# Second chunk of the second layer in seven products, two kinds of transform in attend's bank, folds dealt over more steps

## The chip, the cores and the metric

The kernel runs on one core of one Trainium2 chip. The metric is the device time of one execution in microseconds (us), the median of three runs; less is better. Times that belong to single instructions come from one further execution, which was recorded by the hardware profiler.

## The reference

Two blocks follow each other. The first is attention with a top-k mask over 8 batches, 8 heads, 576 tokens and 64 elements a head; the second mixes tokens and channels by a two-dimensional Fourier transform and then applies a two-layer perceptron. All values are fp32.

```python
scores = scale * np.matmul(q, k.transpose(0, 1, 3, 2))
kth = np.partition(scores, -32, axis=-1)[..., -32:-31]
scores = np.where(scores >= kth, scores, -1e9)
attn = softmax(scores)
x = (attn @ v) as (batch, token, 8 heads * 64)
mixed = np.real(np.fft.fft(np.fft.fft(x, axis=1), axis=2))
u = x + mixed
un = (u - mean(u)) / np.sqrt(var(u) + 1e-06)
out = u + np.maximum(un @ w_ch1, 0.0) @ w_ch2
```

Here w_ch1 is 512 x 2048 and w_ch2 is 2048 x 512.

## The kernel before, in words

**Steps.** The order of all engines' work is written out by a planner in the kernel and kept as written. The unit is a step, and each step i handles one attention tile (128 queries of one head, or the 64 last queries of two heads): there are 9 tiles for a pair of heads, 36 for a batch, 288 in all. A step issues, in this order on PE: scores of tile i+3 (L338, L353, L368), sometimes transposes of q or k (L282), sometimes the transposes of finished output to tokens (tpx, L512), the planned transforms ("pe1", "pe2", "pe"), the transposes of the probabilities of tile i-2 (tpP, L435 and L446), and at certain steps attend (o, L472). Between these pieces PE gets units of the perceptron from a queue, as many as level() and the planner's costs allow; a unit is at most eight or sixteen matmuls. ACT copies scores out of PSUM, makes half of the mask (relu, L405) and the exponential (L414), and copies the transposed probabilities (L438). DVE finds the 32 largest scores by four rounds of MAX8 (L389) and MATCH_REPLACE8 (L391). POOL makes the bounds nt of a tile (L398) and the other half of the mask (a subtraction, L408). In a step POOL's order is: the subtraction, the operations planned under "pool0" (folds), sums that wait in a list (some_sums), the bounds, further sums, and then what is planned under "pool" and "pool2". For pool0 the planner counts 1.5 us an operation; the sums before the bounds get what is left of 2.1 us, and those after it 1.3 us.

**Transforms.** When a batch's attention is complete, its x is folded (sums and differences of mirrored tokens and channels, fold_ops, on POOL for batches 1 to 6), transformed along the tokens (half_of_tokens: yp, L663, two halves g2 for each of two parities), copied to y by ACT (L694 and after), transformed along the channels (dft_channels: mp, L720 and L724, one for each of the five token tiles t), copied to us by ACT (L741), added to x by POOL (L747), measured by DVE (L752), scaled by 1/sqrt (rsqrt, DVE and POOL) and transposed for the perceptron (tpu, L789). The steps of these are set at the end of the kernel from T0, a few steps after the batch's last tile. The transforms of one batch so fall into the steps in which the perceptron of the batch before is finishing.

**Perceptron.** The tokens of a batch are two chunks: chunk 0 holds tiles 0, 1 and the tail tile 4, chunk 1 holds tiles 2 and 3. For each chunk hidden() makes relu(un @ w1) into a tile hT (L874, L878), 16 units. The second layer then has two forms. back() (L901) is the plain one: for a 128-token tile 16 matmuls of 512 columns, in 8 units. fast() is a Strassen-Winograd scheme for the two full tiles of a chunk: seven products p2, p1, p5, p4, p6, p3, p7, each 8 matmuls of 256 columns in two parts (product, L1071). An fp32 matmul of the program appears as two MATMUL instructions in the trace. The operands are mixtures of halves of hT ("21", "11", "12", "22", made by POOL in two halves each, L1016) and of w2, kept in DRAM and brought over by 512 KB transfers (bring, L817, on the queue of SP). The results alternate between the two halves of two PSUM banks named v and w. Of the results the first five are scaled by ACT into spare space (L1041) and added to x by POOL (L1043), the last two are added by DVE (L1029). POOL's mixes and adds stand in the list of sums; need() flushes them up to the one that a product requires. In the kernel before, chunk 0 of batches 1 to 6 and both chunks of batch 7 use fast(); everything else uses back().

**PSUM.** Of eight banks, scores have two (ps_s), transposes two (ps_t), attend and tpx share one (ps_o), and three (ps_m) are handed round by bank(): to hidden, back, the products, yp, mp and tpu. A product's bank is held until its last result is read. In batch 7 yp, mp and tpu use the banks of the attention.

Of the kernel before, what the change touches and what calls it, by code (L numbers as in the profile page):

```python
# [72 lines left out]
def kernel(  # L73
# [55 lines left out]
    def bank(shape, name, hold=False):  # L129
        n = banks_free.pop(0)  # L130
        t = ps_m.tile(shape, F32, name=name, tag=f"m{n}", bufs=1)
        if not hold:
            banks_free.append(n)
            return t
        return t, lambda: banks_free.append(n)

    ident = const.tile([P, P], F32, name="ident", tag="ident")
    fs = const.tile([P, 2, 2, 3, KQ], F32, name="fs", tag="fs")
# [468 lines left out]
    def fold_ops(b, par, eng, space="own"):  # L607

        x = x_of[b]

        if space == "hT":
            sp = batp.tile([P, NIT * CW[0]], F32, name=f"fsp_{b}", tag="hT")

        def buf(n, name, cols=DM):
            if space == "hT":
                return sp[:, 2 * DM * n:2 * DM * n + 2 * cols].rearrange("p (s c) -> p s c", s=2)
            pool, tag = (batp, ("fold_s", "fold_d")) if space == "own" else (attp, ("PT0", "PT1"))
            return pool.tile([P, 2, cols], F32, name=f"{name}_{b}_{par}", tag=tag[n % 2], bufs=1)  # L620

        got = folded[b, par] = []

        def first():
            got.append(buf(0, "sd"))
            op = ALU.add if par == 0 else ALU.subtract
            eng.tensor_tensor(out=got[0], in0=x[:, 0:2, :], in1=x[:, 2:4, :], op=op)

        def second():
            got.append(buf(1, "zw"))  # L630
            fold_halves(eng, got[0], got[1])

        def third(n):
            if n == 0:
                got.append(buf(2, "fg", DM + Q2))
            fold_channels(eng, got[1], got[2][:, :, 0:DM], got[2][:, :, DM:DM + Q2], n)

        def both():
            third(0)
            third(1)  # L640

        return [first, second, both, lambda: third(2)]

    def dft_tokens(b, par):
        for g2 in range(2):
# [3 lines left out]
    def half_of_tokens(b, par, g2):  # L649

        while any(u[2] == "hidden" for u in queue):
            one_unit()
        _, zw, fg = folded[b, par]
        if b not in y_of:
            y_of[b] = batp.tile([P, 4, S], F32, name=f"y_{b}", tag="y")
        y = y_of[b]
        shape, name = [P, 2, KQ], f"yp_{b}_{par}_{g2}"

        yp = ps_t.tile(shape, F32, name=name, tag="tp") if b == B - 1 else bank(shape, name)

        def mm(gg, st, lhsT, rows, table, start=False):

            nc.tensor.matmul(  # L663
                yp[rows, gg, :],
                lhsT=lhsT,
                rhs=fs[:, table, par, st, :],
                start=start,
                stop=st == 2,
                skip_group_check=True,
            )  # L670


        for gg in range(2):
            g = 2 * g2 + gg
            for st in range(3):
                f = fg[:, st] if st < 2 else ftail
                first = gg == 0 and st == 0
                if g2:
                    mm(gg, st, f[:, P * g:P * (g + 1)], slice(0, P), gg, first)
                    continue  # L680
                for h in range(2):
                    c0 = P * g + P // 2 * h
                    mm(gg, st, f[:, c0:c0 + P // 2], slice(P // 2 * h, P // 2 * (h + 1)), h, first)
        if g2 == 0:
            for st in range(3):
                f, c = (fg[:, st], DM + Q0) if st < 2 else (ftail, DM)
                mm(0, st, f[:, c:c + 1], slice(Q0, Q0 + 1), 0)

        mir, back = (
            (slice(HS + 2, S, 2), slice(KQ - 2, 0, -1)) if par == 0  # L690
            else (slice(HS + 1, S, 2), slice(KQ - 2, None, -1))
        )
        y2 = y[:, 2 * g2:2 * g2 + 2, :]
        nc.scalar.copy(out=y2[:, :, par:HS + 1:2], in_=yp[:, :, 0:KQ - par])  # L694
        if g2:
            nc.scalar.copy(out=y2[:, 0, mir], in_=yp[:, 0, back])
        else:
            nc.scalar.mul(out=y2[:, 0, mir], in_=yp[:, 0, back], mul=sg[:, 0:1])
        nc.scalar.mul(out=y2[:, 1, mir], in_=yp[:, 1, back], mul=sg[:, 1 + g2:2 + g2])
        if par == 1 and g2 == 1:  # L700
            tails_of_y(b)
# [6 lines left out]
    def dft_channels(b, t, quick=False):  # L708

        rows, y = ROWS[t], y_of[b]  # L710
        shape, name = [P, 2, DM // 2], f"mp_{b}_{t}"
        mp = ps_s.tile(shape, F32, name=name, tag="sp") if b == B - 1 else bank(shape, name)
        def of(g):
            if t == 4:
                return yt_of[b][:, g].rearrange("p h r -> p (h r)")
            k0 = HS * (t // 2) + P * (t % 2)
            return y[:, g, k0:k0 + P]

        for g in range(2):
            nc.tensor.matmul(  # L720
                mp[0:rows, 0, g:DM // 2:2], lhsT=of(g), rhs=fd[:, g], start=True, stop=True
            )
        for g in range(2, 4):
            nc.tensor.matmul(  # L724
                mp[0:rows, 1], lhsT=of(g), rhs=fd[:, 2 * g - 2:2 * g],
                start=(g == 2), stop=(g == 3),
            )
        if quick:
            xt = two(x_of[b][0:rows, t, :])
            at(now[0], "dve", lambda: nc.vector.tensor_tensor(  # L730
                out=xt, in0=mp[0:rows], in1=xt, op=ALU.add
            ))
            at(now[0], "dve", lambda: stats(b, t))
            return 1.75
        key = (b, t > 1 and t < 4)
        if key not in us_of:
            us_of[key] = batp.tile(
                [P, 2 if key[1] else 3, DM], F32, name=f"us_{b}_{t}", tag="fold_d" if key[1] else "fold_s"
            )
        us = us_of[key][0:rows, CHUNKS[int(key[1])].index(t), :]  # L740
        nc.scalar.copy(out=two(us), in_=mp[0:rows])  # L741
        return 1.75
# [117 lines left out]
    def mlp_units(b):  # L860
# [4 lines left out]
        def hidden(ch, it):  # L865
            w, unT = CW[ch], unT_of[b, ch]
            if ch not in hTs:
                hTs[ch] = batp.tile([P, NIT, CW[0]], F32, name=f"hT_{b}_{ch}", tag="hT")
                hT_of[ch] = hTs[ch].rearrange("p i c -> p (i c)")[:, 0:NIT * w].rearrange(
                    "p (i c) -> p i c", c=w  # L870
                )
            hp = bank([P, CW[0]], f"hp_{b}_{ch}_{it}")
            for dt in range(NDT):
                nc.tensor.matmul(  # L874
                    hp[:, 0:w], lhsT=w1[:, dt, P * it:P * (it + 1)], rhs=unT[:, dt, 0:w],
                    start=(dt == 0), stop=(dt == NDT - 1),
                )
            nc.scalar.activation(out=hT_of[ch][:, it, :], in_=hp[:, 0:w], func=AF.Relu)  # L878
# [10 lines left out]
        def ct_tile():  # L889
            if not cts:  # L890
                cts.append(batp.tile([P, 3, DM], F32, name=f"ct_{b}", tag="fold_s"))
            return cts[0]
# [83 lines left out]
        def fast(ch):  # L976
# [22 lines left out]
                }  # L999

            def room(n):
                return ct_tile().rearrange("p t c -> p (t c)")[:, DH * n:DH * (n + 1)]

            def later(key, us, fn, soon=False):
# [17 lines left out]
            def to_x(t, cols, src, n, then=lambda: None):  # L1022
# [4 lines left out]
                if n is None or last:  # L1027
# [9 lines left out]
                    else:  # L1037
                        late_next.append(add)
                    return
                r = room(n)  # L1040
                nc.scalar.mul(out=r, in_=src, mul=rs[:, t:t + 1])  # L1041
                xt = x[:, t, cols]
# [72 lines left out]
            def p6(part):  # L1115
                need((b, ch, "11", part))
                c = product("w", lo, "11", first, part, False)
                if ch == 0:
                    bring(B12, w2_12, part)
                if part:  # L1120
                    to_x(ta, hi, c, 4)
# [29 lines left out]
        for ch in range(2):  # L1151
# [1 line left out]
                (8 * CW[ch] / 1200.0, lambda ch=ch, it=it: hidden(ch, it), "hidden")  # L1153
                for it in range(NIT)
            ]
            seven = b and ch == 0 or last
            if seven:
                begin, products = fast(ch)
                units.insert(1 - NIT, begin)
# [126 lines left out]
    for b in range(B):  # L1286
# [15 lines left out]
        elif soon:  # L1302
# [3 lines left out]
            for par in range(2):  # L1306
                def folds(par=par, b=b, T0=T0):
                    for n, op in enumerate(fold_ops(b, par, nc.gpsimd)):
                        at(T0 + 1 + 3 * par + min(n, 2), "pool0", op)
                at(T0, "begin", folds)  # L1310
            ft, fc = (T0 + 4, T0 + 7), T0 + 8
        elif not last:
            for n, op in enumerate(fold_tails(b, nc.gpsimd)):
                at(T0 - 2 + n, "pool0", op)
            for par in range(2):
                def folds(par=par, b=b, T0=T0):
                    for n, op in enumerate(fold_ops(b, par, nc.gpsimd)):
                        at(T0 + (6 if par else 1) + n, "pool0", op)
                at(T0, "begin", folds)
            ft, fc = (T0 + 5, T0 + 11), T0 + 12  # L1320
        else:
            for op in fold_tails(b, nc.gpsimd):
                at(T0 - 1, "pool0", op)
# [223 lines left out]
```

## Time and profile before

| what | value |
|---|---|
| median of three runs | 1911.16 us (1910.43 to 1911.83) |
| the profiled execution | 1908.21 us |
| its span, from first to last instruction | 1906.4 us |
| mean granted clock of PE | 0.972 |
| PE busy | 1789.7 us, 94% of the span |
| DVE busy | 1584.5 us, 83% |
| ACT busy | 1210.0 us, 63% |
| POOL busy | 909.8 us, 48% |
| share of PE, DVE, ACT, POOL in the chain that ended last | 74%, 11%, 6%, 4% |

PE is the matrix engine, DVE the vector engine, ACT the scalar engine, POOL is GpSimd and SP only issues transfers. A group of the profile is one line of code on one engine with its tiles, "out<-in", the partitions and elements of each, and a count; after the bar stand the busy time, the mean length of one in ns, the idle time of the engine ahead of the group and what ended it. A line of a timeline begins with start and length in us; idle time before it stands in brackets with its releaser. The ends of matmuls are modelled, so neighbours overlap in the lists, and the distance of two starts is the better measure of what one costs. Up to some 222 us of the trace only the first batch's attention runs, beside the preparation of weights; from 1727 us on only the last batch's transforms and perceptron are left.

### The profile page before, as it was taken

The page shows a single profiled execution, that of the slowest core. Times are in us where ns is not written, and L with a number is a line of the kernel's source. Part 1 is how long each engine was busy: PE and PEld are TensorE (multiplying, and loading weights), DVE is VectorE, ACT ScalarE, POOL GpSimd, SP SyncE. Part 2 cuts the span into 40 slices and gives each one's busy share as a digit, 9 for nine tenths or more (in the row PEclk, how much of TensorE's full clock was granted, in tenths as well). Part 3 has the DMA queues.
Part 4 walks back from the last instruction along what each step waited for, and adds up shares of the span by engine and source line. Part 5 has one row for each costly group of instructions (what it writes and reads, how often), then busy time and mean ns, then how long its engine had stood idle before and what let it go on. Part 6 is the DMA issues. An engine that isn't in the chain of part 4 may idle for free.

```text
span 1906.4 us, 28799 instructions
## 1 busy us (share of the span) xinstructions
PE 1789.7 (94%) x9200; PEld 1181.4 (62%) x9200; DVE 1584.5 (83%) x3301; ACT 1210.0 (63%) x3078; POOL 909.8 (48%) x1278
## 2 busy tenths in 40 slices
PE   6567799999999999999999999999999999999999
PEld 3344465474666756667567656667567656667677
DVE  8999999999999998889899988988899988872110
ACT  6878657676766767757676667666676667652100
POOL 4768643546635464345534464245534464241022
PEclk7778899999999999999999999999999999999999
DMA  5323002311104111130113101140113102030132
GB/s 165 112 86 108 20 13 57 92 55 25 47 7 130 33 25 47 42 108 27 25 47 101 50 20 53 41 114 22 25 47 100 51 19 57 25 103 6 50 105 75
DMA packets 184342, 111.25 MB, mean 58 GB/s; under 512 B 125952, under 2 KB 174208, under 8 KB 184192
## 3 DMA queue, kind: packets, MB, share of 16 engines
q1 hardware_dynamic: 183408, 109.20, 20.3%
q8 instruction: 74, 1.21, 0.3%
q14 instruction: 76, 0.62, 0.1%
q10 hardware_dynamic: 784, 0.21, 0.0%
HBM read 93.63 MB, written 15.73 MB: 57 GB/s over the span
## 4 chain that ended last, share of the span: by engine, by line
PE 74%; DVE 11%; ACT 6%; POOL 4%; issue 2%; DMA 2%; SPq 0%; POOLq 0%; DVEq 0%; ACTq 0%
PE hp L874 25%; PE cp L901 10%; PE o L472 7%; PE tpP L435 5%; PE sp L368 5%; DVE m L389 5%; PE cw L1071 5%; PE cv L1071 4%; DVE wk L391 4%; PE yp L663 3%; PE cp L940 3%; PE sp_t L338 2%; POOL wk L408 1%; ACT wk L414 1%; ACT wk L405 1%
## 5 line engine op out<-in xcount | busy, mean ns | idle before, releaser
L408 POOL TENSOR_TENSOR wk<-S,wk 128x576 f32<-128x576 f32 x288 | 408.9, 1420 | 730.8 <-ACT wk L405 697.3
L389 DVE MAX8 m<-wk 128x8 f32<-128x576 f32 x864 | 626.7, 750 | 6.1
L874 PE MATMUL hp<-unT,w 128*128 128x256 f32 (+1 forms) x2048 | 540.3, 411 | 2.6 <-ACT unT L792 2.6
L874 PEld LDWEIGHTS hp<-unT,w 128*128 128x128 f32 x2048 | 374.8, 191 | 124.8 <-issue 26.0
L391 DVE MATCH_REPLACE8 wk<-m,wk 128x576 f32<-128x576 f32 x576 | 427.7, 743 | 0.0
L414 ACT ACTIVATE wk<-wk,nt 128x576 f32<-128x576 f32 x288 | 225.0, 781 | 79.0 <-POOL wk L408 78.0
L405 ACT ACTIVATE wk<-S,nt 128x576 f32<-128x576 f32 x288 | 227.0, 788 | 34.1 <-POOL nt L398 32.9
L435 PE MATMUL tpP<-ident,wk 128*128 128x128 f32 x1152 | 183.4, 283 | 68.5 <-ACT wk L414 44.5
L901 PE MATMUL cp<-w,hT 128*128 128x512 f32 x512 | 240.6, 598 | 0.0
L438 ACT COPY PT<-tpP 128x512 f32<-128x512 f32 (+1 forms) x320 | 171.3, 547 | 106.2 <-PE tpP L435 103.8
L435 PEld LDWEIGHTS tpP<-ident,wk 128*128 128x128 f32 x1152 | 140.4, 145 | 143.7 <-ACT wk L414 67.9
L878 ACT ACTIVATE hT<-hp 128x320 f32<-128x320 f32 (+1 forms) x256 | 105.0, 410 | 195.2 <-PE hp L874 193.0
L389 DVE MAX8 m<-S 128x8 f32<-128x576 f32 x288 | 213.9, 743 | 6.8 <-ACT S L342 6.8
L391 DVE MATCH_REPLACE8 wk<-m,S 128x576 f32<-128x576 f32 x288 | 213.8, 742 | 0.0
L472 PE MATMUL o<-PT,v 128*64 128x256 f32 (+3 forms) x1440 | 193.3, 411 | 2.0 <-ACT PT L438 1.9
L371 ACT COPY S<-sp 128x512 f32<-128x512 f32 (+1 forms) x264 | 141.8, 588 | 50.7 <-PE sp L368 50.3
L368 PE MATMUL sp<-kT,qT 64*128 64x512 f32 (+1 forms) x528 | 161.2, 669 | 5.0 <-ACT means L1259 3.3
L472 PEld LDWEIGHTS o<-PT,v 128*64 128x64 f32 x1440 | 110.6, 151 | 72.8 <-issue 15.7
L901 PEld LDWEIGHTS cp<-w,hT 128*128 128x128 f32 x512 | 88.8, 190 | 86.3 <-issue 86.2
L1016 POOL TENSOR_TENSOR hT<-hT 128x512 f32<-128x512 f32 x64 | 81.5, 1276 | 100.1 <-ACT hT L878 88.4
L1071 PE MATMUL cw<-w,hT 128*128 128x256 f32 x448 | 106.7, 383 | 1.9 <-POOL nt L398 1.2
L1071 PEld LDWEIGHTS cw<-w,hT 128*128 128x128 f32 x448 | 81.4, 190 | 19.4 <-issue 5.2
(157 smaller groups left out, 2178.8 us busy)
## 6 DMA issues: line engine op xcount, KB each, us to landing
w<-w_parts SPq DMA_DIRECT2D x82, 512.0 KB, 4.5
space<-in_moe_w_ch_dram SPq DMA_DIRECT2D x32, 512.0 KB, 3.4
nat<-in_q_dram SPq DMA_DIRECT2D x128, 64.0 KB, 2.2
v<-in_v_dram SPq DMA_DIRECT2D x128, 64.0 KB, 2.2
out_dram<-x SPq DMA_DIRECT2D x32, 256.0 KB, 2.1
nat<-in_k_dram SPq DMA_DIRECT2D x124, 64.0 KB, 2.2
w_parts<-w_t SPq DMA_DIRECT2D x8, 512.0 KB, 2.9
w_s<-w_parts SPq DMA_DIRECT2D x8, 512.0 KB, 5.0
```

What stands on the lines that cost most here:

```text
L368: nc.tensor.matmul(sp[r], lhsT=qT[hd, q_cols], rhs=kT[hd, :], start=True, stop=True)
L389: ops.append(lambda src=src, m8=m8: nc.vector.max(out=m8, in_=src))
L391: ops.append(lambda src=src, m8=m8: nc.vector.match_replace(w, m8, src, NEG))
L405: nc.scalar.activation(out=w, in_=Ssb[i], func=AF.Relu, scale=-FAR, bias=Nt[i][:, 1:2])
L408: nc.gpsimd.tensor_tensor(out=w, in0=Ssb.pop(i), in1=w, op=ALU.subtract)
L414: nc.scalar.activation(out=w, in_=w, func=AF.Exp, bias=Nt.pop(i)[:, 0:1], accum_out=den_t[pair % 3][:, c:c + 1],)
L435: nc.tensor.transpose(tp[:, c, :], p_sb[:, k0 + P * c:k0 + P * (c + 1)], ident)
L438: nc.scalar.copy(out=pt[:, NF * he:NF * (he + 1), col:col + w], in_=tp[:, :, o:o + w])
L472: nc.tensor.matmul(o[D * e:D * (e + 1), c0:c1], lhsT=vv[:, c, e, :], rhs=pt[:, 2 * NF if c == NF else NF * e + c, c0:c1], start=(c == 0), ...
L874: nc.tensor.matmul(hp[:, 0:w], lhsT=w1[:, dt, P * it:P * (it + 1)], rhs=unT[:, dt, 0:w], start=(dt == 0), stop=(dt == NDT - 1),)
L901: nc.tensor.matmul(cp, lhsT=hT[:, it, P * n:P * (n + 1)], rhs=w2[:, it, :], start=(it == 0), stop=(it == NIT - 1),)
L1071: nc.tensor.matmul(dst, lhsT=h()[a][:, kc, :], rhs=rhs_of(kc), start=start and kc == 0, stop=kc == NK - 1, skip_group_check=True,)
```

## The change

There are three edits. First, seven is true for every batch but the first, so that chunk 1 of batches 1 to 6 takes fast() too (chunk 1 of batch 7 already did); for chunk 1 the room for scaled results is the spare end of its own hT tile, which is as large as that of chunk 0, result 4 reuses the room of result 0 and so needs the latter's add first, hidden() flushes the open sums when it takes a new hT tile, and p6 brings a mixture of w2 again at the end of every chunk but the very last. Second, bank_of_o() gives the second halves of the token transforms and two of the five channel transforms a tile of attend's bank, in steps where the position in the pair of heads allows it, for batches 1 to 6. Third, the fold's third operation is split: three lambdas in the order 0, 2, 1 in place of both() and the last; the steps are dealt anew, for batches 2 to 6 the second parity starts at T0 + 7 in place of T0 + 6 and the first token transform at T0 + 6 in place of T0 + 5.

```diff
+    def bank_of_o(shape, name, steps):
+        if now[0] % PER_PAIR in steps:
+            return ps_o.tile(shape, F32, name=name, tag="o")
+        return bank(shape, name)
...
-        def both():
-            third(0)
-            third(1)
-
-        return [first, second, both, lambda: third(2)]
+        return [first, second] + [lambda n=n: third(n) for n in (0, 2, 1)]
...
-        yp = ps_t.tile(shape, F32, name=name, tag="tp") if b == B - 1 else bank(shape, name)
+        if b == B - 1:
+            yp = ps_t.tile(shape, F32, name=name, tag="tp")
+        else:
+            yp = bank_of_o(shape, name, (0, 1, 4, 5, 6) if g2 and b else ())
...
-        mp = ps_s.tile(shape, F32, name=name, tag="sp") if b == B - 1 else bank(shape, name)
+        if b == B - 1:
+            mp = ps_s.tile(shape, F32, name=name, tag="sp")
+        else:
+            mp = bank_of_o(shape, name, (0, 1, 4, 5, 6, 7) if t in (1, 4) and b else ())
...
             if ch not in hTs:
+                for s in list(sums):
+                    need(s[0])
                 hTs[ch] = batp.tile([P, NIT, CW[0]], F32, name=f"hT_{b}_{ch}", tag="hT")
...
             def room(n):
+                if ch:
+                    n0 = NIT * CW[1] + DH * (n % 4)
+                    return hTs[1].rearrange("p i c -> p (i c)")[:, n0:n0 + DH]
                 return ct_tile().rearrange("p t c -> p (t c)")[:, DH * n:DH * (n + 1)]
...
+                if ch and n == 4:
+                    need((b, ch, "x", 0))
                 r = room(n)
...
-                if ch == 0:
+                if not (last and ch):
                     bring(B12, w2_12, part)
...
-            seven = b and ch == 0 or last
+            seven = b > 0
...
-                        at(T0 + 1 + 3 * par + min(n, 2), "pool0", op)
+                        at(T0 + 1 + 3 * par + (0, 1, 1, 2, 2)[n], "pool0", op)
...
-                        at(T0 + (6 if par else 1) + n, "pool0", op)
+                        at(T0 + (7 if par else 1) + (0, 1, 2, 2, 3)[n], "pool0", op)
                 at(T0, "begin", folds)
-            ft, fc = (T0 + 5, T0 + 11), T0 + 12
+            ft, fc = (T0 + 6, T0 + 11), T0 + 12
```

## The prediction

> **What bounds the kernel now.** First the page's busy times and 40 slices, then the windows of engine busy time, the groups by shape, and the timelines of single engines.
>
> ```profile
> PE 1789.7 (94%) x9200; PEld 1181.4 (62%) x9200; DVE 1584.5 (83%) x3301; ACT 1210.0 (63%) x3078; POOL 909.8 (48%) x1278
> PE   6567799999999999999999999999999999999999
> DVE  8999999999999998889899988988899988872110
> ```
>
> From slice 7 on PE is busy at 90% or more in every slice, but DVE shows nines too, one group per batch. Windows (us, then busy and count of PE, PEld, DVE, ACT, POOL) separate them; the first two together are one batch's period (the end of batch 4's perceptron, batch 5's transforms, then its perceptron), the last is the tail:
>
> ```profile
> 1213.00:1369.00 156.00, 155.61 (x829) 103.11 (x828) 134.62 (x275) 100.31 (x257) 79.25 (x114) 1.00 0.21 56
> 1369.00:1419.00 50.00, 48.72 (x266) 32.22 (x264) 48.61 (x106) 38.57 (x99) 23.39 (x39) 1.00 0.15 42
> 1727.00:1906.00 179.00, 175.25 (x788) 128.76 (x786) 28.07 (x69) 25.28 (x63) 24.58 (x33) 1.00 0.19 63
> ```
>
> For 156 us PE has no gap and DVE has 21 us to spare: PE work removed there shortens the kernel. In the 50 us after it (the steps behind each batch's second token transform) DVE is busy 48.6 and PE merely nearly so: PE work removed there is worth little, and work moved in costs. The tail is PE alone.
>
> Now the matrix work concerned. Line 901 is the plain product back(), line 1071 the seven products, 1016 their mixes on POOL, 1041 the scaling on ACT, 1043 POOL's add:
>
> ```profile
> L901 PE MATMUL cp<-w,hT 128*128 128x512 f32 x512 | 240.6, 598 | 0.0
> L1016 POOL TENSOR_TENSOR hT<-hT 128x512 f32<-128x512 f32 x64 | 81.5, 1276 | 100.1 <-ACT hT L878 88.4 <-PE cw L1071 8.0 <-PE cz L1071 3.7
> L1043 POOL TENSOR_TENSOR x<-x,ct 128x256 f32<-128x256 f32 x30 | 21.7, 733 | 2.8 <-ACT ct L1041 2.7
> L1041 ACT ACTIVATE ct<-cw,gi 128x256 f32<-128x256 f32 x18 | 8.5, 473 | 12.3 <-PE cw L1071 12.0
> ```
>
> A mean of 598 ns is no price, since successive matmuls overlap. The pitch is, from starts in PE's timeline: 20 plain ones from 1775.55 to the next group at 1784.14, so 0.4295 each, and 16 small ones in 3.455 us, so 0.216.
>
> ```profile
> 1775.55 8.75 PE L901 MATMUL cp<-w,hT 128*128 128x512 f32 x20
> 1784.14 6.08 PE L874 MATMUL hp<-unT,w 128*128 128x320 f32 x22
> ...
> 1818.59 3.62 PE L1071 MATMUL cv<-w,hT 128*128 128x256 f32 x16
> 1822.05 3.62 PE L1071 MATMUL cw<-w,hT 128*128 128x256 f32 x16
> ```
>
> **What the Trainium skill says.** "Perfetto Trace Analysis", Optimization Strategy: kernels can have several regimes, in which the most contended engine changes. The two windows agree (155.6 of 156 on PE, 48.6 of 50 on DVE). "PSUM — Partial Sum Buffer", PSUM bank collisions raise a hardware error: guard PSUM by bank, not by address. Two products share a bank here, and the trace agrees: product p6 (0.39 us of wait, below) begins only after ACT has read the other half. Same page, Engine vs sequencer instructions: GpSimd's queue is strict FIFO. The trace agrees in so far as POOL's groups stand in program order. "SBUF — State Buffer", two separate sides: GpSimd and a two-input DVE operation contend for one port pair. I bound that at 0: the large DVE operations here read one tensor, and MATCH_REPLACE8 takes 0.74 us in the DVE-bound stretch with POOL half busy.
>
> **1. Products, chunk 1 of batches 1 to 6.** A chunk is 64 plain matmuls in the trace (2 tiles x 16 x 2): 64 x 0.4295 = 27.5 us. Seven products are 7 x 8 x 2 = 112 small ones: 112 x 0.216 = 24.2. Gain 3.3 a chunk, six chunks 19.8. So line 901 must fall to 128 matmuls and line 1071 grow by 672.
>
> Where the gain lands, from the order of the two built programs, counting PE's units between like transposes: batch 1 3.3, batch 2 3.3, batch 3 1.6 in the PE-bound part and 1.7 inside a DVE-bound stretch, batch 4 3.3, batch 5 3.3 but with 2.2 us of units moved into the next DVE-bound stretch, batch 6 5.4 (with those units back). So 1.7 is lost at once, less some 0.4 that DVE's own gaps there give back: **1.3**. The 2.2 moved in meet a PE that is at 97% already; half of what doesn't fit shows: **0.8** (bounds 0 and 2.2).
>
> **2. New waits of PE.** (a) p6 follows p4 in one bank and may not write before ACT has scaled p4's half. Chunk 0 shows it:
>
> ```profile
> 1036.27 1.89 PE L1071 MATMUL cw<-w,hT 128*128 128x256 f32 x8
> 1038.00 0.39 PE L338 MATMUL sp_t<-kt,qT 128*128 128x128 f32 x2
> 1038.77 1.53 PE L1071 MATMUL cw<-w,hT 128*128 128x256 f32 x6 [0.39 <-POOL nt L398]
> ...
> 1037.43 0.78 ACT L414 ACTIVATE wk<-wk,nt 128x576 f32<-128x576 f32 x1 [0.37 <-POOL wk L408]
> 1038.20 0.47 ACT L1041 ACTIVATE ct<-cw,gi 128x256 f32<-128x256 f32 x1
> ```
>
> The scaling begins when the exponential before it is off ACT, lasts 0.47, and p6 starts 0.1 later; the releaser named (POOL nt) had long been done. There 0.39 us of a score matmul lies between. In the built order of after, p4 and p6 are adjacent in batches 2, 4 and 5: nothing covers 0.47 + 0.1, and the exponential in front (0.78 + 0.1 reading its sum) may be running. From 0.57 to 1.45: I take **1.3 x 3**. In batch 6's tail no exponential is near: 0.6 + 0.1 = **0.7**. In batch 3 four transposes (0.6) and more lie between: 0. Batch 1, where the order differs: 0.
>
> (b) p3's second part needs half 1 of mix "12". On POOL it stands behind a mask subtraction and a fold. A step of POOL before:
>
> ```profile
> 1356.50 0.19 POOL L398 TENSOR_TENSOR nt<-m,cc 128x2 f32<-128x2 f32 x1
> 1359.89 1.41 POOL L408 TENSOR_TENSOR wk<-S,wk 128x576 f32<-128x576 f32 x1 [3.20 <-ACT wk L405]
> 1361.25 0.20 POOL L398 TENSOR_TENSOR nt<-m,cc 128x2 f32<-128x2 f32 x1
> ```
>
> PE's step began at 1356.85 (score matmul); the subtraction ended 4.4 us later, as it waits for ACT's relu. In after (step 229 for batch 4) the fold's third part (1.85) and the bound (0.2) follow, then the mix (1.28): ready at 4.4 + 1.85 + 0.2 + 1.28 = 7.7 after the step's start. PE asks for it at 5.8, by its place in the built order and the pitches. Wait **1.9 x 3** (batches 2, 4, 5); bounds 0, if the relu comes in 2 us earlier as in steps where the idle before it was 1 us, and 4. In batch 3 the folds lie elsewhere: 0.6 here and 0.7 at p7: **1.3**. Batch 1 none. Sum of (a) and (b): 3.9 + 0.7 + 5.7 + 1.3 = **11.6**.
>
> **3. Other engines.** POOL gains per chunk 8 mixes x 1.276 + 5 adds x 0.733 less one 1.274 add of before: 12.6 us, to about 104 of a 214 us batch; its own time is covered, its order is what (b) prices. ACT gains 1.7 us a batch (five scalings of 0.47 less one of 0.63), covered: it has 55 us idle in the 156. DVE gains one 256-wide add, 0.48, where it has room. SP issues 12 more 512 KB transfers a batch, 4.5 us to landing, asked for at least one step (6 us) ahead; q, k and v loads queued behind them are issued some 25 us ahead: **0**; if that cover fails, 0.5 each as at the 0.5 us wait for w_parts now.
>
> **4. Banks.** Second token halves and two of five channel transforms use attend's bank. Attend, or the transform, then waits for a copy (0.43 for y, 0.64 for us). I find one such wait of about 0.4 and one of 0.6 a batch in batches 2 to 6; most lies in the DVE-bound stretch. Five times 0.2: **1.0** (bounds 0 and 5). Against it the freed bank lets the token transform keep pace: nothing that PE waits for now.
>
> **5. Folds.** From batch 2 on only the time moves; fold waits there are nil. In batch 1 PE waits 3.4 us on fg now (1.8 + 1.6), beside a DVE that is nearly full: **-0.5**.
>
> Sum: -19.8 + 1.3 + 0.8 + 11.6 + 1.0 - 0.5 = **-5.6**: more than half of the products' gain goes into their own waits. The profiled execution took 1908.2 us, 1906.4 of it the span; it becomes 1902.6. The median of the runs, 1911.16, is 3.0 above it: **1905.5**.
>
> **Rivals.** *A, the waits hardly appear.* ACT's scaling comes before the exponential is ready (0.6 x 3 in place of 3.9), and POOL idles 1 to 3 us a step ahead of its subtraction, in which mixes find room: (b) 2 in place of 7. Then -19.8 + 1.3 + 0.8 + 2.5 + 2 + 1 - 0.5 = -12.7: 1898.4; with nothing lost, 1891.4. For it: chunk 0's products cost only 1.9 us of waits in the whole kernel now. Against: chunk 0's products have no folds beside them.
>
> *B, POOL becomes the bound around the folds: slower.* Steps 227 to 229 of batch 4 now hold mix + subtraction + second fold (1.28 + 1.41 + 2.5 + 0.2 = 5.4), mix + subtraction + third parts (1.28 + 1.41 + 3.15 + 0.2 = 6.0) and mix + subtraction + last part (4.7). A PE step is 214.8 / 36 = 6.0. It decides once the relu holds POOL for over 0 us in the full step and 0.6 in the one before; in the timeline such idle is 1 to 3 us. Then the bound nt comes late, with it relu, exponential and PE's transposes of that step, and p3 waits 6 instead of 1.9: 4 us more in each of batches 2 to 5, 16 in all: -5.6 + 16 = +10: 1921.6. Against it: POOL runs a step behind without harm, as nt is used a step later.
>
> *C, no net effect:* the PE time saved returns as idle PE before DVE's stretch, since scores then come earlier but DVE, at 86%, takes them late: 1911. Against: in the 156 us window it is DVE that waits (5.17 us for PE before 1369.27).
>
> **How the numbers follow.** About 0.2% (3.8 us) can be told from no change here. Forecast -1 to -10: 0.56, of which 0.40 is beyond 3.8 us; A 0.22; B 0.17; C 0.05. Faster 0.40 + 0.22 = 0.62; within 0.15 + 0.05 = 0.20; slower 0.01 + 0.17 = 0.18. Range: A's upper half and the weak form of B (+4): 1893 to 1915; below lies some 0.05, above 0.15. Cases faster alone: 1893 to 1908.
>
> **What would show it.** In the profile of after: line 901 at x128, cv and cw up by 672 together; PE gaps of about 1.3 at the first cw of p6 (behind ACT ct) and 1.9 at cv of p3 (behind POOL hT) in batches 2, 4, 5; the DVE-bound stretches no longer and no shorter; the tail shorter by over 3; no wait on fg or on a transfer. Gaps before p3 of 5 us, or transposes waiting for the exponential in steps 228 to 230, would mean B; p3 without gaps A. Wrong altogether if the PE-bound windows don't shrink.

## The result and the profile after

The changed kernel takes 1925.24 us (median of four runs, 1924.73 to 1926.17) against 1911.49 of the kernel before: ratio 1.0073, 95% interval 1.0056 to 1.0090. It is 13.8 us slower, where 6 faster was forecast. The profiled execution took 1926.17, its span is 1924.4, 18.0 longer than that of before. Some 4 of these 18 belong to the two executions that were profiled: that of before took 3.3 less than its median, that of after 0.9 more (the last section shows one source of such differences).

First the page of after: busy times, and the head of the chain that ended last, in which POOL's share has grown from 4% to 10%.

```profile
PE 1782.8 (93%) x9488; PEld 1241.7 (65%) x9488; DVE 1593.8 (83%) x3307; ACT 1217.8 (63%) x3102; POOL 981.8 (51%) x1350
PE 65%; DVE 11%; POOL 10%; ACT 8%; issue 4%; DMA 2%; SPq 0%; POOLq 0%; DVEq 0%; ACTq 0%
```

The groups by shape, of the lines that take the place of 901, 1071 and 1016:

```profile
L910 PE MATMUL cp<-w,hT 128*128 128x512 f32 x128 | 61.0, 600 | 0.0
L1085 PE MATMUL cw<-w,hT 128*128 128x256 f32 x832 | 199.9, 385 | 9.4 <-POOL fg L564 4.5 <-issue 3.2 <-POOL hT L1028 0.8
L1085 PE MATMUL cv<-w,hT 128*128 128x256 f32 x672 | 159.8, 383 | 5.6 <-POOL hT L1028 5.6
L1028 POOL TENSOR_TENSOR hT<-hT 128x512 f32<-128x512 f32 x112 | 143.4, 1282 | 115.8 <-ACT hT L887 92.5 <-PE cw L1085 19.1 <-PE cz L1085 3.7
```

The work moved as the diff says: 384 plain matmuls fewer, 384 + 288 = 672 small ones more, 48 mixes more. What is new stands behind the bars: 15 us of waits of the products, where before had 1.9. And the same three stretches as before, cut at about the same work (to the end of batch 4's products, the stretch that DVE bounds, the tail):

```profile
1221.00:1379.50 158.50, 154.49 (x874) 111.44 (x872) 137.46 (x280) 101.82 (x264) 88.47 (x122) 1.00 0.32 88
1379.50:1432.50 53.00, 49.50 (x263) 34.01 (x262) 48.09 (x103) 38.53 (x98) 26.10 (x43) 0.97 0.20 59
1744.00:1924.00 180.00, 174.07 (x842) 139.13 (x840) 32.87 (x70) 26.86 (x68) 37.43 (x45) 1.00 0.29 92
```

The first was 156.0 us with 0.4 us without PE, and now has 4 us of gaps; the second was 50, and PE's clock in it is no longer 1.00; the tail has 6 us without PE where it had 4.

To see where the 18 us come from I took, for every matmul in both traces, the time from its start to the next start; what the quickest quarter of that shape needs counts as work, the rest as wait. After less before, by attention tiles (36 a batch):

| tiles | what runs there | work | wait |
|---|---|---|---|
| 72 to 84 | transforms of batch 1 | 0 | +6.3 |
| 84 to 112 | perceptron | -3.4 | +1.1 |
| 112 to 132 | products of batch 1, transforms of 2 | +0.2 | +3.9 |
| 132 to 152 | perceptron | -3.4 | -0.9 |
| 152 to 160 | products of batch 2, transforms of 3 | +0.1 | +4.6 |
| 160 to 184 | perceptron | -1.7 | 0 |
| 184 to 196 | products of batch 3, transforms of 4 | +0.2 | +2.7 |
| 196 to 224 | perceptron | -5.1 | +1.9 |
| 224 to 232 | products of batch 4, transforms of 5 | +0.1 | +4.5 |
| 232 to 240 | DVE bounds | -2.7 | +3.4 |
| 240 to 256 | perceptron | +1.0 | +0.6 |
| 256 to 268 | products of batch 5, transforms of 6 | -1.5 | +4.8 |
| 268 to 276 | DVE bounds | +2.2 | -0.2 |
| 276 to the end | last batch | -5.4 | +4.8 |

The sum is -19.6 of work and +37.5 of wait (the other 72 tiles add nothing). So the saving is real and as large as forecast, but 37.5 us stand against it, where the forecast set 14.2 against it in all. The question is which of the three edits made the other 23.

### The profile page after: what moved, and what is told of

Read it like the earlier page. It is cut to its first block, busy times and chain, and to the rows that moved or that the text cites. A ratio compares the mean times of both kernels' runs of the same rounds, so it can differ in the third digit from the quotient of the medians.

```text
span 1924.4 us, 29582 instructions
## 1 busy us (share of the span) xinstructions
PE 1782.8 (93%) x9488; PEld 1241.7 (65%) x9488; DVE 1593.8 (83%) x3307; ACT 1217.8 (63%) x3102; POOL 981.8 (51%) x1350
## 4 chain that ended last, share of the span: by engine, by line
PE 65%; DVE 11%; POOL 10%; ACT 8%; issue 4%; DMA 2%; SPq 0%; POOLq 0%; DVEq 0%; ACTq 0%
PE hp L883 24%; PE cw L1085 7%; PE o L477 6%; PE cv L1085 6%; DVE m L394 5%; PE tpP L440 5%; PE sp L373 4%; DVE wk L396 4%; POOL wk L413 3%; PE cp L949 3%; PE yp L667 3%; POOL fg L564 2%; PE sp_t L343 1%; ACT wk L419 1%; POOL hT L1028 1%
## 5 line engine op out<-in xcount | busy, mean ns | idle before, releaser
L1085 PE MATMUL cw<-w,hT 128*128 128x256 f32 x832 | 199.9, 385 | 9.4 <-POOL fg L564 4.5
L1028 POOL TENSOR_TENSOR hT<-hT 128x512 f32<-128x512 f32 x112 | 143.4, 1282 | 115.8 <-ACT hT L887 92.5
L1085 PEld LDWEIGHTS cw<-w,hT 128*128 128x128 f32 x832 | 152.5, 191 | 40.6 <-issue 11.9
L1085 PE MATMUL cv<-w,hT 128*128 128x256 f32 x672 | 159.8, 383 | 5.6 <-POOL hT L1028 5.6
L1085 PEld LDWEIGHTS cv<-w,hT 128*128 128x128 f32 x672 | 122.6, 190 | 34.6 <-issue 10.6
```

The costliest lines, as they stand in the source:

```text
L1028: nc.gpsimd.tensor_tensor(out=v[dst][:, k], in0=v[a][:, k], in1=v[c][:, k], op=op)
L1085: nc.tensor.matmul(dst, lhsT=h()[a][:, kc, :], rhs=rhs_of(kc), start=start and kc == 0, stop=kc == NK - 1, skip_group_check=True,)
```

## The experiments

My theory after the result: the folds of batch 1 are dealt in a worse order, the products cost what was predicted, and some waits cost more than their length, as PE's clock falls to half after them. The rivals: attend's bank is the loss; the products themselves are.

**1. Each edit alone.** The kernel before with the third edit alone:

```diff
+        return [first, second] + [lambda n=n: third(n) for n in (0, 2, 1)]
...
+                        at(T0 + (7 if par else 1) + (0, 1, 2, 2, 3)[n], "pool0", op)
...
+            ft, fc = (T0 + 6, T0 + 11), T0 + 12
```

> The kernel before with the third edit alone (folds split and dealt anew). Theory 1: in batch 1 the order 0, 2, 1 puts the part that the first half of the token transform reads last, so PE waits for it; the trace of after loses 5.9 us between tiles 79 and 86, some 1.2 of it to half-clock matmuls that follow a long wait: 5 to 6 us slower than before, 1916 to 1918, and up to 3 more if the later first transform of the other batches costs too. Theory 2 (the folds are as neutral as predicted, and what is lost there comes from attend's bank): 1911 +- 1.

Measured 1926.94 against 1911.74, ratio 1.0079 (1.0056 to 1.0101): 15 us, all of the loss of the whole change and more than either theory allowed. The two profiled executions lie 20.6 apart, and the trace shows it in steps: 6.6 us in batch 1, then 3.7 to 3.8 in the transforms of each of batches 2, 5 and 6 (2.0 in batch 4, 1.0 in batch 3). Of the 6.6 only 1.0 is a longer wait for the folds; most of the rest lies in three stretches at half clock, and the profiled execution of before has none at these tiles. PE in batch 5's transforms (timeline of that kernel, which has other line numbers):

```profile
1352.73 0.66 PE L353 MATMUL sp<-kT,qT 64*64 64x256 f32 x8
1355.18 0.49 PE L338 MATMUL sp_t<-kt,qT 128*128 128x128 f32 x2 [1.78 <-ACT S L360]
1355.50 3.56 PE L897 MATMUL cp<-w,hT 128*128 128x512 f32 x4
```

and ACT ahead of that wait:

```profile
1352.40 0.42 ACT L690 COPY y<-yp 128x290 f32<-128x290 f32 x1 [0.71 <-PE yp L659]
1352.71 0.30 ACT L692 COPY y<-yp 128x143 f32<-128x143 f32 x1
1352.88 0.41 ACT L695 ACTIVATE y<-yp,sg 128x143 f32<-128x143 f32 x1
1353.15 0.59 ACT L438 COPY PT<-tpP 128x512 f32<-128x512 f32 x1
1353.62 0.81 ACT L414 ACTIVATE wk<-wk,nt 128x576 f32<-128x576 f32 x1
1354.29 0.22 ACT L414 ACTIVATION_READ_ACCUMULATOR wk<-wk,nt 128x1 f32 x1
1354.38 1.50 ACT L360 COPY S<-sp 64x256 f32<-64x256 f32 x4
```

The same step in before, PE and then ACT:

```profile
1338.30 0.66 PE L353 MATMUL sp<-kT,qT 64*64 64x256 f32 x8
1338.89 1.98 PE L901 MATMUL cp<-w,hT 128*128 128x512 f32 x4
1340.71 0.38 PE L338 MATMUL sp_t<-kt,qT 128*128 128x128 f32 x2
...
1339.07 1.52 ACT L360 COPY S<-sp 64x256 f32<-64x256 f32 x4 [1.03 <-PE sp L353]
```

T0 + 6 is the step just ahead of the one that scores the 64-query tile. In before ACT is idle when these scores come, and begins to copy them 0.77 us after their first matmul. Now the six copies to y stand ahead on ACT's queue, which pushes the copy of the probabilities and the exponential into this place as well: the four score copies begin 1.65 us after the first matmul, both score banks are full, and PE waits 1.78 us. There is a second part, which the edit brings with it: the four matmuls of the perceptron that lie between the scores and sp_t in before come behind the wait here, as the planner deals the perceptron's units around the transform. No run separates the two. The four matmuls take 3.56 us where four of these take 1.88 to 1.98 in the trace of before: that is half clock (the mean granted clock was 0.63 from 1354.5 to 1358.5), 1.7 us more. Batch 4 has the same wait of 1.78 us without half clock behind it, hence its 2.0. No wait of PE for POOL, where the edit was made, is new in these batches.

The second edit alone, the two functions with bank_of_o put into the kernel before:

> The kernel before with the second edit alone (yp and mp in attend's bank). Theory 1: 0.3 to 0.6 us of waits a batch, partly beside a full DVE: 1911 to 1913.5. Theory 2 (attend's bank is the main loss, as attend, the tokens' transposes and two transforms then wait for each other's readers): 1918 or more.

Measured 1912.33, ratio 1.0002 (0.9993 to 1.0010). The rival with attend's bank as the loss falls. The first edit alone:

> The kernel before with the first edit alone (chunk 1 in seven products, the transforms left with the one bank that the two held ones leave them). Theory 1: PE's work falls by 19.8 us, the waits of products p6 and p3 give back 11.6, and the rest shows how much comes from the interplay with transforms that have one bank: 1905 to 1912. Theory 2 (the products themselves lose, POOL's mixes delaying the masks): 1918 or more.

Measured 1922.38, ratio 1.0060 (1.0043 to 1.0076): slower, as theory 2 had it. But in the trace of the products alone p3 waits 2.23 us and more follows it (half clock, then 1.05 us in which the second half of the token transform waits for ACT to empty the one bank left). The three edits alone cost 15.2 + 0.6 + 10.6 = 26.4 us and together 13.8, so they don't add up; what the products need of the other two is asked below.

**2. The folds put back in two steps.** In the changed kernel, first batch 1:

```diff
-        return [first, second] + [lambda n=n: third(n) for n in (0, 2, 1)]
+        return [first, second] + [lambda n=n: third(n) for n in ((0, 1, 2) if b == 1 else (0, 2, 1))]
-                        at(T0 + 1 + 3 * par + (0, 1, 1, 2, 2)[n], "pool0", op)
+                        at(T0 + 1 + 3 * par + (0, 1, 2, 2, 2)[n], "pool0", op)
```

> The changed kernel with batch 1's folds as in the kernel before, order 0, 1, 2 and the old steps; all else as after. Theory 1: 5 to 6 us of the loss go, 1919 to 1920. Theory 2: nothing changes, 1925.

Measured 1923.36: 1.9 us, and 3.6 between the two profiled executions; the sign is as expected, the size a third to two thirds of it. The place is where it was expected. PE in before, then in after:

```profile
468.38 0.46 PE L663 MATMUL yp<-fs,fg 128*64 128x145 f32 x2 [0.32 <-POOL fg L559]
469.67 0.59 PE L663 MATMUL yp<-fs,fg 128*64 128x145 f32 x5 [0.82 <-POOL fg L573]
```

```profile
470.18 0.46 PE L667 MATMUL yp<-fs,fg 128*64 128x145 f32 x2 [1.22 <-POOL fg L564]
471.46 0.58 PE L667 MATMUL yp<-fs,fg 128*64 128x145 f32 x5 [0.81 <-POOL fg L578]
```

The end of all three parts on POOL is the same to 0.2 us in both, but the transform's first half reads part 1, which 0, 2, 1 puts last. Then the first transform of batches 2 to 6, both in the kernel before (folds dealt anew, but T0 + 5 kept) and in the changed one:

```diff
-            ft, fc = (T0 + 6, T0 + 11), T0 + 12
+            ft, fc = (T0 + 5, T0 + 11), T0 + 12
```

> The kernel before with the third edit, but batch 1's folds as before and the first token transform of batches 2 to 6 left at T0 + 5. Theory 1: what the folds edit loses in batches 2 to 6 (3.7 us each in batches 4 to 6 in the trace of the edit alone) comes from the first transform one step later: its copies to y stand on ACT ahead of the score copies of the step with the 64-query tile, PE waits 1.8 us for a score bank, and its clock then runs at half for 3 us. With the transform back: 1911.7 +- 1.5. Theory 2 (POOL loses by the later folds themselves): 1916 or more.

> The changed kernel with batch 1's folds as before and the first token transforms at T0 + 5. Theory 1: against the kernel with only batch 1's folds put back (1923.4) batch 2 gains 3.4 us (wait 1.8, half clock 1.6), and 1.5 more where p6 is no longer adjacent to p4 in batch 4: 1918 to 1920. Theory 2 (the first transform then meets folds that aren't finished, and waits for them): 1923 or more.

Measured 1910.40, ratio 0.9997 (0.9989 to 1.0004), and 1915.69, ratio 1.0019 (1.0011 to 1.0027). The one step of the first transform is the whole loss of the folds from batch 2 on: dealing the folds anew is neutral by itself (of the 3.7 us that the expectation puts in batches 4 to 6, batch 4 had only 2.0). In the changed kernel it is worth 7.7 us, more than the 5 expected. There the wait for a score bank is left in batch 2 alone:

```profile
702.02 0.49 PE L343 MATMUL sp_t<-kt,qT 128*128 128x128 f32 x2 [1.79 <-ACT S L365]
```

The rest of the 7.7 comes by other ways. Against the trace with only batch 1 put back, 3.3 us are gone at tiles 196 to 256, where a wait of 2.13 with half clock behind it became one of 1.03 without; 1.0 to 1.3 in each of the products of batches 2 and 5, where p6's wait of 1.5 became one of 0.8; and 1.2 in batch 2's transforms. So the edit's worth in this kernel is measured, but it isn't the score bank for the most part.

**3. The products' two waits.** PE in the changed kernel, batch 4's products:

```profile
1360.05 1.89 PE L1085 MATMUL cw<-w,hT 128*128 128x256 f32 x8
1363.42 1.97 PE L1085 MATMUL cw<-w,hT 128*128 128x256 f32 x8 [1.47 <-POOL fg L564]
...
1373.01 1.99 PE L1085 MATMUL cv<-w,hT 128*128 128x256 f32 x8 [1.71 <-POOL hT L1028]
```

ACT ahead of the first, and POOL ahead of the second:

```profile
1362.09 0.78 ACT L419 ACTIVATE wk<-wk,nt 128x576 f32<-128x576 f32 x1 [1.19 <-POOL wk L413]
1362.77 0.19 ACT L419 ACTIVATION_READ_ACCUMULATOR wk<-wk,nt 128x1 f32 x1
1362.87 0.45 ACT L1055 ACTIVATE hT<-cw,gi 128x256 f32<-128x256 f32 x1
```

```profile
1368.35 1.42 POOL L413 TENSOR_TENSOR wk<-S,wk 128x576 f32<-128x576 f32 x1 [1.82 <-ACT wk L410]
1369.72 1.70 POOL L564 TENSOR_TENSOR fg<-fg 128x128 f32<-128x128 f32 x4
...
1371.68 1.27 POOL L1028 TENSOR_TENSOR hT<-hT 128x512 f32<-128x512 f32 x1
```

p6 starts 0.1 us after ACT's scaling (1362.87 + 0.45), whatever releaser the line names, and p3 0.06 after the mix. To separate p6 from p4, on top of the kernel with folds and transforms put back:

```diff
+            if got and queue[0][2] == "apart":
+                break
             got += one_unit()
...
-                (1.75, lambda f=f, part=part: f(part), "back")
+                (1.75, lambda f=f, part=part: f(part),
+                 "apart" if f is p6 and part == 0 and ch and not last else "back")
```

> The same as the kernel with folds and first transforms put back, with p6 begun only behind another piece of PE's work than p4 (batches 2 and 5 change). Theory 1: ACT's scaling of p4 is covered there, 1.5 us a batch: 3 us faster than that kernel. Theory 2 (PE's idle time there is filled from a slack, as DVE decides after these steps): within 1 us of it.

Measured 1911.58, 4.1 us faster than the kernel beside it; the trace gives 1.8 in each of the two batches that the edit changes. To bring the mixes ahead of the mask subtraction:

```diff
-        some_sums(1.3)
+        some_sums(2.6)
...
+        some_sums(2.6 if i >= 2 * PER_BATCH and i % PER_BATCH in range(5, 13) else 1.3)
```

The first form stands on the kernel with folds and transforms put back, the second on the one with p6 apart.

> The same as the kernel with folds and first transforms put back, and two mixes instead of one allowed on POOL right behind each step's bounds (2.6 us in place of 1.3). Theory 1: the mix that p3 waits for stands behind a mask subtraction, for which POOL idles 1 to 3 us; ahead of it, p3's 1.7 us in three batches go: 3 to 5 us faster than that kernel, 1914 to 1916. Theory 2 (POOL is the bound around the folds): the subtractions come later, and with them the exponentials: 2 or more slower than that kernel.

> The kernel with p6 apart (1911.6), and two mixes behind the bounds only in the steps of the folds (5 to 12 of each 36, from batch 2's period on). Theory 1: in the trace of the kernel with early mixes everywhere these steps gained 0.8, 0.4, 1.5, 3.0 and 0.4 us, and lost 2 in batch 4's stretch that DVE bounds and 3 in the tail; without the tail's loss 2 to 4 faster than p6 apart: 1908 to 1910. Theory 2 (what PE gains before the stretch that DVE bounds is lost in it): within 1 of 1911.6.

Both missed: 1917.32 (1.6 slower than the kernel without it, in runs from 1910.31 to 1920.74) and 1915.97 (4.4 slower than p6 apart). The waits of p3 did go, 3.0 us in batch 4's products and 1.5 in batch 3's; but the stretch that DVE bounds took them back and more, +2.0 and +4.1 at tiles 232 to 236, and in the second kernel +2.6 behind batch 3's products. The tail, where the last batch's transforms wait for DVE's folds, lost 3.0 and 3.7 more. At tile 234 PE arrives earlier than before and waits 3.04 and 3.43 us for an exponential that hardly comes earlier; half clock followed the second of these waits, not the first.

**4. Where products earn nothing.** Batch 1's second chunk left plain, alone and with the early mixes:

```diff
-            seven = b > 0
+            seven = b > (1 if ch else 0)
```

> The kernel with p6 apart, and batch 1's second chunk plain as in the kernel before. Theory 1: DVE bounds that period throughout, so the products' 3.3 us are worth nothing there while their waits (some 3.5 us in steps 118 to 124) count: 1.5 to 2.5 faster, 1909 to 1910. Theory 2 (the chunk earns its 3.3): 3 slower, 1915.

> Both edits together, the early mixes and batch 1's second chunk plain. Theory 1: 1906 to 1909, faster than the kernel before by over 2 us. Theory 2: 1911 to 1912.

Measured 1910.22 and 1908.67. The first is 1.4 faster than with the chunk in products, less than the spread of single runs, and the ratio to the kernel before is 0.9999 for both; so the chunk earns nothing, and that it costs isn't shown. The second is the first version ahead of the kernel before: ratio 0.9985 (0.9977 to 0.9993). Its trace shows batch 3 gaining 3.0 by the early mixes and losing 5.1 behind:

```profile
1183.94 1.11 PE L440 MATMUL tpP<-ident,wk 128*128 128x128 f32 x4 [3.65 <-ACT wk L419]
1184.84 4.41 PE L883 MATMUL hp<-unT,w 128*128 128x320 f32 x8
```

The same place with one mix a step:

```profile
1184.95 0.66 PE L440 MATMUL tpP<-ident,wk 128*128 128x128 f32 x4 [1.05 <-ACT wk L419]
1185.45 2.32 PE L883 MATMUL hp<-unT,w 128*128 128x320 f32 x8
```

PE is done with what stands ahead at 1180.29 (1183.94 - 3.65) in place of 1183.90 (1184.95 - 1.05), 3.6 us earlier, and the transposes begin 1.0 earlier; then half clock takes 2.1 us (4.41 against 2.32 for eight). What holds the exponential stands on POOL's queue, here in the kernel with the early mixes: the first line of a block, and behind the block the mask subtraction.

```profile
1177.01 0.20 POOL L778 TENSOR_TENSOR t<-gi 128x5 f32<-128x5 f32 x1 [2.69 <-DVE gi L774]
...
1181.58 1.41 POOL L413 TENSOR_TENSOR wk<-S,wk 128x576 f32<-128x576 f32 x1 [0.17 <-issue]
```

The sixteen small operations of rsqrt start when DVE has measured the batch's last tile, and take 4.4 us; the subtraction, which the exponential needs, stands behind them. The same block stands ahead of the waits at tile 234 above, and in before too (there PE waits 0.41 us). The 3.6 us that PE saved brought it forward by only 1.2 (in the kernel with one mix a step it starts at 1178.24). A kernel with the subtraction ahead of it was not run. So the early mixes were kept in batches 2 and 5 alone, with batch 6's chunk in products and plain:

```diff
+        some_sums(2.6 if i % PER_BATCH in range(5, 13) and i // PER_BATCH in (4, 7) else 1.3)
...
+            seven = b > 0 and (ch == 0 or b in (2, 3, 4, 5, 7))
```

> The kernel with both edits (1908.7), with the early mixes only in the steps of batch 2's and batch 5's products. Theory 1: early mixes gain 1.8 us each there; in batch 3's steps they gained 3.0 and then lost 5.1 in the stretch that DVE bounds, 2.2 of it to half clock: without them there, 2 faster: 1906 to 1907. Theory 2 (that loss was chance): 3 slower, 1911 to 1912.

> The same, and batch 6's second chunk plain as well. Theory 1: the last batch's folds on DVE set when its token transforms may start, and what PE saves ahead of them becomes a wait (4.4 us of waits against 5.2 of work in the trace): within 1.5 us of the kernel beside it. Theory 2 (the tail is PE alone, as the prediction had it): 3.3 slower.

Measured 1907.63, ratio 0.9978 (0.9969 to 0.9987), and 1907.71, ratio 0.9982 (0.9973 to 0.9990). The first is 1.0 faster than with early mixes in batch 3 too, half of what was expected and within the spread of runs, though its trace has the 5.1 us of that place back and gives up the 3.0. Batch 6's chunk earns nothing: the tail isn't PE alone. Between the two traces 3.3 us of work come back as 2.6 of waits, 0.9 of them for DVE's last fold, 0.6 of p6, 0.5 for transfers. In after, PE waits for the same fold, which in before was ready in time behind more plain work (there the transform begins at 1747.54 without a wait):

```profile
1767.51 0.46 PE L667 MATMUL yp<-fs,fg 128*64 128x145 f32 x2
1768.92 0.59 PE L667 MATMUL yp<-fs,fg 128*64 128x145 f32 x5 [0.94 <-DVE fg L578]
```

**5. Attend's bank, with the products.** p6 apart, with the transforms in the one bank that the products leave:

> The kernel with p6 apart, and the transforms in the one bank that the products leave, as in the kernel before (no tile of theirs in attend's bank). Theory 1: attend's bank costs 0.6 us of waits a batch, and saves the wait of the token transform's second half for the copy of its first (1.05 us in each of five batches in the trace of the products alone): 2 slower, 1913 to 1915. Theory 2 (attend's bank is a burden): 2 or more faster.

Measured 1922.94: 11.4 us slower than with it. The direction is theory 1's, the size over five times it. The waits of that kernel name the places; in the kernel beside it they are 1.1 and 1.6 us in all:

```profile
PE yp L659 <- ACT y L695: 6.3, 6, 1.1
PE mp L716 <- ACT us L737: 3.7, 2, 1.9
```

## Why the prediction was wrong, by its own steps

- **Step 1, the gain.** The size holds: 19.6 us of PE's work against 19.8. "Where the gain lands" failed. Batch 1's chunk was counted with 3.3 and earns nothing (0 to 1.4 faster without it); the tail, "PE alone", was counted with 5.4, and its own chunk earns nothing (0.1). What was counted in full in batches 3 and 4 stands ahead of a stretch that DVE bounds, and the early mixes show that a gain there is paid back in the stretch, where POOL's rsqrt, begun by DVE, holds the exponential; that the products' gain there was lost in the same way is argued from this, not shown. Busy time alone didn't tell these stretches: PE's 48.72 of 50 us stood beside DVE's 48.61.
- **Step 2a, p6.** Right: 1.49, 1.47 and 1.50 against 1.3 in batches 2, 4 and 5, 0.6 in the tail against 0.7. Undoing it gave 1.8 a batch in two of them. Not foreseen: in batch 1's chunk 0 a product now waits 1.45 us for ACT's scaling in the same way, which none there did in before.
- **Step 2b, p3.** Right in batches 2, 4 and 5: 1.71 each against 1.9. Batch 3 has 0.52 + 0.43 against 1.3. Batch 1 has none, as forecast; with the folds and the first transform put back its products wait 0.55 and 1.80.
- **Step 3.** Right: PE waits 1.8 us for transfers of w2 in all, as much as before, with 72 such transfers more.
- **Step 4, the banks.** The cost fits (0.6 measured alone, within noise of 0; 1.0 forecast). "Against it the freed bank lets the token transform keep pace: nothing that PE waits for now" was mis-sized. It is true of the kernel before; with two banks held by products, attend's bank is worth 11.4 us.
- **Step 5, the folds: the step that failed.** It priced the folds' operations and their readiness on POOL, found the time neutral, and took batch 1 as a gain of 0.5. Alone the edit costs 15 us. Two lines of the diff cost, and the step weighed neither: the order 0, 2, 1, without asking which part is read first, and the first transform's move by one step, without following its ACT copies past the score copies of the next step, or PE's other work around it. In the changed kernel the two are worth 1.9 and 7.7; of the 7.7 the score bank is a part, and how the rest comes about is shown place by place above, not as one cause.
- **What no step had: the clock.** Every wait was priced at its length. Behind the first 300 us PE ran at half clock for 20.5 us in after and for 6.8 in before; where PE is busy, up to half of that is lost.

From the forecast to the result: 1905.5, plus 2.4 for batch 1's folds (+1.9, not -0.5), plus 7.7 for the transform's step, plus 4.7 for batch 1's chunk (3.3 + 1.4), plus 3.4 for the tail's, makes 1923.7 of 1925.2. The terms were measured in different kernels, in which such edits don't add up, and the 1.4 isn't clear of noise: the sum says where the miss lies, and that it comes so close is in part luck.

Of the rivals, B gave the nearest time for a reason that doesn't show: p3 waits 1.7 us, not 6, and POOL's folds are ready. A and C fail, C only as a whole: its mechanism, saved PE time coming back as idle time of PE around DVE's stretch, was set aside because DVE waited for PE at the stretch's start, and is what the early mixes met inside it. The page "Perfetto Trace Analysis", Optimization Strategy, which the prediction cited for the two regimes, names regimes that change over time, and the two stretches agree; what it doesn't say, and the early mixes show, is that work saved in one regime has to be asked about in the next.

## What to carry to other kernels

A transform, copy or fold that is moved by one step moves all that it queues on every engine: follow each of those instructions to what now stands behind it, above all on ACT, which here holds PE's score banks. PE time that is saved counts only if the next thing that PE waits for also comes earlier; ahead of a stretch that another engine bounds it didn't here. Price a wait of PE of nearly 2 us at up to twice its length. Try edits that belong together in one kernel before dropping one that brings nothing alone: attend's bank was worth 0 without the products and 11 us with them.

## What the runs showed that was not expected

**Waits and the clock.** The clock granted to PE has two values in these traces, 1.00 and 0.50. It changes only at the marks of a grid of 3.41 us, which lies differently in each execution, and behind the first 300 us each stretch at half clock lasts one or two intervals of it (3.41 or 6.83 us; those that the end cuts off aside). In the sixteen traces I took PE's idle time in each interval at full clock behind those 300 us. Of 39 intervals with over 1.9 us idle, all were followed by half clock in the next one; of 23 with 1.77 to 1.9, 10 were; of the other 7406, 9 were, eight of them at one place (tile 80, with 0.8 us idle), which I can't explain.

So it isn't the length of a wait alone: it is how much of it falls into one interval. All sixteen traces have a wait of 2.28 us at tile 77. In twelve at least 2.17 of it lies in one interval, and half clock follows; in four the grid cuts it so that no interval has over 1.90, and it doesn't. This makes some 2 us between executions (2.3 at tiles 72 to 84 between the kernel with p6 apart, which is among the twelve, and the one beside it, which is not; their code is alike there). The profiled execution of before is one of the four. PE ahead of and in attend there, in the kernel with attend's bank alone and in the kernel before:

```profile
476.49 1.06 PE L440 MATMUL tpP<-ident,wk 128*128 128x128 f32 x4 [2.28 <-ACT wk L419]
477.48 4.14 PE L477 MATMUL o<-PT,v 128*64 128x320 f32 x20
```

```profile
476.93 0.66 PE L435 MATMUL tpP<-ident,wk 128*128 128x128 f32 x4 [2.28 <-ACT wk L414]
477.51 2.91 PE L472 MATMUL o<-PT,v 128*64 128x320 f32 x20
```

The two intervals of the grid in each (the second number is the length, the third PE's busy time, the third from the end the granted clock):

```profile
473.17:476.59 3.42, 1.14 (x11) 0.95 (x10) 2.27 (x5) 3.03 (x12) 2.68 (x3) 1.00 0.01 2
476.59:480.00 3.41, 3.41 (x14) 1.80 (x16) 3.23 (x7) 2.32 (x6) 2.47 (x2) 0.50 0.02 5
```

```profile
472.98:476.39 3.41, 1.67 (x15) 1.48 (x13) 2.88 (x5) 2.65 (x10) 3.31 (x3) 1.00 0.01 3
476.39:479.80 3.41, 2.87 (x22) 1.70 (x24) 2.58 (x6) 2.33 (x7) 1.82 (x2) 1.00 0.03 5
```

The Trainium skill, "TensorE: Matmul & The Clock Gate", What's actually happening, says that the clock falls to half after an idle window of about 3.4 us, and that the window runs free of the kernel. The free-running window agrees, with 3.41 us here and another offset in each execution. But a window doesn't have to be idle throughout: 1.78 us without PE in one were enough in several places, and the measurement decides.
